# A fused attention-and-MLP kernel: slot-side softmax transposed without its normalisation, the slot reads divided by the sums afterwards

## The chip, the cores and the metric

The kernel runs on one core of a Trainium2 chip. The metric is the device time of one execution in microseconds, the median of several; lower is better.

## The reference

For each of B = 8 batches and H = 8 heads, `x` is [512, 64] and `state` is [32, 64]. Tokens read from the state slots and slots read from the tokens; both results are concatenated to 544 rows per batch, and the heads side by side give 512 columns. A two-layer network with the activation s r^2 + b follows. In short:

```python
scores  = x @ state.T / 8;   xread = softmax(scores, over slots) @ state
scores2 = state @ x.T / 8;   sread = softmax(scores2, over tokens) @ x
X = concat([xread, sread])               # 8 batches x 544 rows, 512 columns
r = relu(X @ w_in)                       # w_in [512, 2048]
out = (s * r * r + b) @ w_out            # w_out [2048, 512]
```

`scores2` is the transpose of `scores`, so one matrix of exponentials E serves both softmaxes: column sums give the token side, row sums give the slot side.

## The kernel before, in words

Slots stand on the partitions: four heads of 32 slots make 128 partitions, the 512 tokens are the columns, and two groups g = 0, 1 hold the eight heads. For each batch b:

- `T_mm` writes the scores (T) to PSUM, and `E_exp` on ScalarE makes E[g] = exp(T / 8) in fp16 with `accum_out`, which leaves the sums over tokens in `rs`, one column for each half of the tokens.
- Token side: `D_mm` multiplies E by a block matrix of ones (D), `D_ln` and `D_exp` on ScalarE make R = 1/D, and `a4_mul` on VectorE makes a4 = E R, the normalised weights. `M_mm` forms M = state @ w_in, four column chunks c of 512 for each batch, cast to fp16 by `M_cast` on ScalarE or VectorE. `h_mm` then multiplies a4 by M: h(b,f), f = 0 to 15, are blocks of 128 hidden units for 512 tokens, each of two matmuls of 512 columns.
- Slot side: `q_rec` adds the two halves of `rs` and takes the reciprocal q, `a2_mul` on VectorE multiplies E by q, `aT_dma` on SP transposes the product (aT), `V_mm` multiplies aT by x (V, in PSUM), `V_copy` casts V to `sr`, and `sr_dma` on SP transposes sr into `srdT`. When all eight batches have done so, `h_mm` with the name "sr" runs the slot rows through w_in itself.
- The network's second half: `relu` (ScalarE mostly), `square` (VectorE) make g. Batch 0 is multiplied by w_out directly in groups of four f: `rows_mm`, here called rows(b, rr, part), each four matmuls of 512 columns, closed by `rows_out` on VectorE. The other batches, and the slot rows, use a seven-product scheme: `pair_sums` (pd) and `weight_sum` (u) on VectorE, `step_mm` on TensorE with 256-column matmuls, `step_out` on VectorE (c), `step_put` to memory.

Batches 0 and 1 arrive as fp32 on SP's queue and are cast and transposed on the engines (`cast_x`, `xT_mm`, `xT_copy`). Everything else is loaded by GpSimd's queue, which casts on the way; its order is the string `SEQ`: four chunks of w_in (wi), four of w_out (wo), 512 KB each as fp16, then x of batches 2 and 3.

The order of instructions on each engine is not written down by hand. The class `Plan` holds every operation with an engine, a guessed duration, a key, what it needs and makes and which buffers it takes, and lays them out greedily by ready time and key; `after` is an earliest time. The constants `K` set the keys. The result is only an order: on the chip each engine runs its queue in that order and waits on semaphores, and nothing holds an operation back until its planned time. PSUM has four banks for attention tiles (T, D, M, V and the transposes share the pool "att"), two for h and two for outputs; the four are handed out again in the order in which they were given back.

T_mm, M_mm, V_mm and the bias sum run TensorE in tiles of 32 columns or 64 rows; the others use the full array. The prediction calls a run of such tiled products, between others, an excursion. "warm" matmuls are fillers that the plan puts into TensorE's queue before 14 us.

The kernel's core for the slot side:

```python
nc.vector.tensor_scalar(a[f"a2{g}"], a["E"][g], a["q"][:, g : g + 1], None, ALU.mult)   # a2_mul
nc.sync.dma_start_transpose(a["aT"][:, g], a[f"a2{g}"])                                 # aT_dma
copy_on(e, A[b]["sr"], A[b]["V"].rearrange("p g d -> p (g d)"))                         # V_copy
```

## Time and profile before

| | us |
|---|---|
| median of 5 runs | 212.17 (211.1, 211.1, 212.17, 212.8, 212.9) |
| profiled execution, its own time | 211.49 |
| its span, first to last instruction | 209.7 |
| TensorE busy | 201.5 |
| VectorE busy | 174.7 |
| ScalarE busy | 138.0 |
| GpSimd busy | 42.0 |

The granted TensorE clock was 0.998 of full speed. In the profile, PE is TensorE's matmuls, PEld its weight loads, DVE VectorE, ACT ScalarE, POOL GpSimd, SP the queue that issues most transposes. A line such as "L213 PE MATMUL h<-a,M" names the line of the code (L213 is the helper `mm`), the engine, and the tiles written and read. "Busy" adds an instruction's whole duration; two neighbours on ScalarE or VectorE overlap by about a tenth of a microsecond, so the spacing of their starts is shorter than the duration.

### The profile page before, as it was taken

To read this page: it belongs to the slowest core of one execution; us is meant where nothing else is said; L and a number is where in the kernel's file an instruction comes from. 1 tells how busy PE (TensorE), PEld (TensorE's weight loads), DVE (VectorE), ACT (ScalarE), POOL (GpSimd) and SP (SyncE) were. 2 spreads that over 40 slices of the span, in tenths; PEclk is the share of its full clock that TensorE was granted. 3 is DMA by queue.
4 is the path that set the end of the run, shared out by engine and by line. 5 is a ranking of instruction groups with operands and counts; after the bars stand their busy time and mean duration, and the time that the engine had idled before them with its cause. 6 is when DMAs were issued, how large, how long until landed. Compare 5 with 4: busy or idle time off the path is not lost.

```text
span 209.7 us, 4984 instructions
## 1 busy us (share of the span) xinstructions
PE 201.5 (96%) x1961; PEld 131.2 (63%) x1961; DVE 174.7 (83%) x415; ACT 138.0 (66%) x311; POOL 42.0 (20%) x65
## 2 busy tenths in 40 slices
PE   7896999999999999999999999999999999999993
PEld 3432434435667676667767667766766777888882
DVE  2489899998799998999998998989898988828872
ACT  4797999814986698868695959675967554116500
POOL 0760000262050224013231214111101111200000
PEclk9999999999999999999999999999999999999999
DMA  6999999579759764952495449741212110320132
GB/s 202 293 181 206 208 211 147 118 174 169 154 122 131 128 158 95 127 134 73 77 149 107 112 100 140 96 125 53 75 34 100 50 53 28 105 76 3 53 125 75
DMA packets 42344, 25.00 MB, mean 119 GB/s; under 512 B 26448, under 2 KB 40528, under 8 KB 42320
## 3 DMA queue, kind: packets, MB, share of 16 engines
q0 software_dynamic: 12896, 14.68, 36.4%
q1 hardware_dynamic: 29136, 9.84, 23.7%
q8 instruction: 15, 0.25, 0.5%
q10 hardware_dynamic: 288, 0.16, 0.3%
q14 instruction: 9, 0.07, 0.1%
HBM read 17.33 MB, written 8.91 MB: 125 GB/s over the span
## 4 chain that ended last, share of the span: by engine, by line
PE 86%; DMA 7%; DVE 3%; POOL 1%; SPq 0%; ACT 0%; issue 0%
PE o L213 47%; PE h L213 25%; DMA wi<-in_moe_w_in_dram 5%; PE Mps L213 4%; PE h_sr L213 3%; PE osr L213 3%; DMA xf<-in_x_dram 2%; DVE g L810 2%; PE V L213 1%; PE D L213 1%; PE T L213 1%; PE wsum_ps L213 0%; SPq L255 0%; POOL wi L361 0%; POOL wo L371 0%; DVE osb L953 0%
## 5 line engine op out<-in xcount | busy, mean ns | idle before, releaser
L804 ACT ACTIVATE g<-h 128x512 f16<-128x512 f32 x125 | 73.0, 601 | 31.1 <-PE h L213 29.9
L213 PE MATMUL h<-a,M 128*128 128x512 f16 x256 | 73.9, 379 | 0.0
L810 DVE TENSOR_TENSOR g<-g 128x512 f16<-128x512 f16 x128 | 52.1, 425 | 4.2 <-ACT g L804 2.8
L213 PEld LDWEIGHTS <-pd 128*128 128x128 f16 x448 | 43.0, 98 | 18.3 <-issue 2.6
L213 PEld LDWEIGHTS <-g 128*128 128x128 f16 x400 | 38.4, 98 | 23.2 <-issue 2.6
L213 PE MATMUL o<-u,pd 128*128 128x256 f16 x336 | 45.8, 273 | 0.0
L213 PE MATMUL o<-wo,g 128*128 128x256 f16 (+1 forms) x288 | 45.5, 296 | 0.2 <-DVE osb L953 0.2
L1061 POOL DMA_DIRECT2D out_dram<-c x24 | 16.4, 683 | 102.6 <-DVE c L1049 97.6
L305 ACT CAST M<-Mps 128x512 f16<-128x512 f32 x51 | 28.7, 594 | 7.6 <-PE Mps L213 7.2
L213 PEld LDWEIGHTS <-M 128*128 128x128 f16 x256 | 24.3, 98 | 10.9 <-issue 3.1
L1049 DVE SCALAR_TENSOR_TENSOR c<-o,sb_cols,bias_bc 128x512 f32<-128x512 f32 x28 | 21.0, 749 | 6.1 <-PE o L213 5.5
L1049 DVE SCALAR_TENSOR_TENSOR c<-o,sb_cols,c 128x512 f32<-128x512 f32 x21 | 15.8, 751 | 5.7 <-PE o L213 5.2
L826 DVE TENSOR_TENSOR pd<-g 128x1024 f16<-128x1024 f16 x28 | 19.2, 686 | 0.3
L213 PE MATMUL o<-u,g 128*128 128x256 f16 x112 | 15.7, 273 | 0.0
L548 ACT ACTIVATE E<-T 128x256 f16<-128x256 f32 x32 | 11.9, 385 | 4.9 <-PE T L213 4.9
L213 PE MATMUL o<-wo,pd 128*128 128x256 f16 x112 | 15.0, 273 | 0.0
L384 POOL DMA_DIRECT2D xn<-in_x_dram x18 | 13.9, 813 | 0.0
L837 DVE TENSOR_TENSOR pd<-g,pd 128x512 f16<-128x512 f16 x28 | 11.8, 422 | 0.5
L793 ACT ACTIVATE g_sr<-h_sr 128x128 f16<-128x128 f32 x16 | 4.4, 277 | 11.8 <-PE h_sr L213 11.8
L835 DVE TENSOR_TENSOR pd<-g,pd 128x512 f16<-128x512 f16 x28 | 11.8, 420 | 0.3
L574 ACT ACTIVATE R<-D 128x512 f16<-128x512 f32 x16 | 9.6, 597 | 0.5
L567 ACT ACTIVATE D<-D 128x512 f32<-128x512 f32 x16 | 9.5, 595 | 0.0
(78 smaller groups left out, 164.7 us busy)
## 6 DMA issues: line engine op xcount, KB each, us to landing
out_dram<-c POOLq DMA_DIRECT2D x24, 256.0 KB, 2.5
xf<-in_x_dram SPq DMA_DIRECT2D x8, 256.0 KB, 5.3
wi<-in_moe_w_in_dram POOLq DMA_DIRECT2D x4, 512.0 KB, 11.5
wo<-in_moe_w_out_dram POOLq DMA_DIRECT2D x4, 512.0 KB, 14.9
xn<-in_x_dram POOLq DMA_DIRECT2D x16, 128.0 KB, 3.6
xn<-in_x_dram POOLq DMA_DIRECT2D x2, 512.0 KB, 14.7
out_dram<-osb POOLq DMA_DIRECT2D x4, 256.0 KB, 3.2
out_dram<-c SPq DMA_DIRECT2D x4, 256.0 KB, 2.4
```

Of the source, the lines that this page charges most:

```text
L213: return nc.tensor.matmul(out, lhsT, rhs, start=start, stop=stop, tile_position=tp, is_transpose=is_transpose, skip_group_check=True,)
L305: nc.scalar.copy(dst, src)
L384: nc.gpsimd.dma_start(out=xn[b][:, h0:h1].rearrange("p h c d -> p h (c d)"), in_=x[b, h0:h1].rearrange("h (q c) d -> q h (c d)", q=P),)
L548: nc.scalar.activation(a["E"][g][:, 256 * m : 256 * m + 256], a["T"][m][:, g, :], AF.Exp, scale=scale, accum_out=a["rs"][:, g, m : m + 1],)
L574: nc.scalar.activation(A[b][f"R{g}"], A[b][f"D{g}"], AF.Exp, scale=-1.0)
L804: nc.scalar.activation(g_of(name, f), OSB["h", name, f], AF.Relu)
L810: ENG[e].tensor_mul(g_of(name, f), g_of(name, f), g_of(name, f))
L826: nc.vector.tensor_tensor(pd[:, :, 0:2], g4[:, :, 1:2, :].to_broadcast((P, 2, 2, t)), g4[:, :, 0:4:3, :], ALU.subtract,)
L835: nc.vector.tensor_tensor(pd[:, :, 2], g4[:, :, 3], pd[:, :, 0], ALU.subtract)
L837: nc.vector.tensor_tensor(pd[:, :, 3], g4[:, :, 2], pd[:, :, 2], ALU.subtract)
L1049: nc.vector.scalar_tensor_tensor(t, src, s_bc, add, ALU.mult, ALU.add)
L1061: ENG[e].dma_start(dst[:, rows:SCH:2, hD * h : hD * h + hD], SN[b, name])
```

## The change

E itself is transposed, not E q. `a2_mul` and its tiles are gone, `V_copy` multiplies by q on its way out of PSUM. For batches 0 and 1 the exponentials no longer accumulate; instead `E_sum` on ScalarE reads each E tile later with a Copy that accumulates, its output unused. There are four E buffers for each g instead of three, and four q. The load order and all keys are others, so the order of every engine's queue is other too. The transpose's `after` is now `K["a2"]` + 2 g.

```diff
--- before.py
+++ after.py
@@ -128,6 +128,7 @@
                     if kind == "load":
                         done = max(channel, end + 2.0) + span
                         channel = max(channel, done)
+                        done += 0.8
                     elif kind == "tp" and e == "SP" and now < channel + 4.0:
                         done = end + max(span, min(8.0, 6.0 - 0.75 * (now - channel)))
                         channel = max(channel, now + 2.0) + 1.1
@@ -273,12 +274,12 @@
         xn[b] = xpool.tile([P, H, SCH, D], FP16, name=f"xn_{b}", tag="xn")
 
     K = dict(
-        h1=10.0, hs=1.7, M0=-5.0, M1=2.6, T1=1.9, x2=11.8, T2=30.2, D2=21.8, M2=30.7, V0=21.7, V1=28.2, u=16.2,
-        us=7.8, pd1=8.7, o0=13.5, o2=20.2, w=38.4, r=-3.3, T=-9.7, D=1.8, Mb=8.9, V=11.6, S=3.7, S0=2.2,
-        E=-13.4, L=-7.1, E0=-7.3, L0=-7.0, E1=-0.2, L1=-6.1, a4=4.0, Mc=5.2, pd=14.0, solo=5.4, f0=-0.5,
-        f1=15.2, mc=0.2, hsr=-5.9, Ssr=-0.1, jE00=-8.0, jE01=3.2, jL00=1.3, jL01=1.0, jR00=-2.8, jR01=0.3,
-        jE10=3.3, jE11=7.2, jL10=-6.0, jL11=7.6, jR10=7.2, jR11=-3.9, jM0=2.4, jM1=1.3, xc=-10.2, a2=30.7,
-        lx=8.3, la=12.9, lb=7.4,
+        h1=11.4, hs=0.6, M0=-4.5, M1=1.5, T1=-0.1, x2=24.5, T2=21.0, D2=30.7, M2=36.0, V0=28.2, V1=21.7, u=8.1,
+        us=10.1, pd1=2.0, o0=16.0, o2=26.0, w=25.1, r=0.5, T=-11.4, D=7.3, Mb=3.9, V=7.6, S=3.4, S0=-1.2,
+        E=-7.1, L=-5.0, E0=-6.7, L0=6.1, E1=-7.0, L1=-5.1, a4=-9.7, Mc=4.9, pd=14.6, solo=6.8, f0=0.4, f1=15.4,
+        mc=0.9, hsr=-10.9, Ssr=-2.4, jE00=-6.1, jE01=5.2, jL00=3.0, jL01=14.6, jR00=-0.1, jR01=-6.7, jE10=3.3,
+        jE11=-6.4, jL10=-5.2, jL11=5.1, jR10=-1.5, jR11=7.4, jM0=0.0, jM1=0.3, xc=-8.5, a2=30.8, lx=6.3, la=7.6,
+        lb=9.4, rs=28.3,
     )
     A = {b: {"E": {}, "a4": {}} for b in range(B)}
     G, PD, U, SN, OSB = {}, {}, {}, {}, {}
@@ -308,9 +309,9 @@
 
     plan = Plan(
         {
-            "att": 4, "h": 2, "xn": 6, "xT": 2, "stT": 2, "E0": 3, "E1": 3, "R0": 1, "R1": 1,
-            "a40": 2, "a41": 2, "M": 2, "aT": 3, "a20": 2, "a21": 2, "sr": 4, "g": 8, "pd": 7,
-            "u": 4, "osb": 6, "q": 2, "rs": 3,
+            "att": 4, "h": 2, "xn": 6, "xT": 2, "stT": 2, "E0": 4, "E1": 4, "R0": 1, "R1": 1,
+            "a40": 2, "a41": 2, "M": 2, "aT": 3, "sr": 4, "g": 8, "pd": 7,
+            "u": 4, "osb": 6, "q": 4, "rs": 3,
         },
         solo=K["solo"],
     )
@@ -390,7 +391,7 @@
 
     gate = konst.tile([P, 2], FP16, name="gate")
     nc.gpsimd.tensor_copy(gate, xf_part(0, 2)[:, 0, 0:2])
-    SEQ = "wi0 wo0 wi1 wi2 wo1 wo2 wi3 wo3 x2 x3"
+    SEQ = "wi0 wi2 wo1 wi1 wo0 wi3 wo2 wo3 x2 x3"
     seq = [(t[:-1], int(t[-1])) for t in SEQ.split()]
     for n, it in enumerate(seq):
         key = -40 + n
@@ -543,15 +544,20 @@
             a = A[b]
             if "rs" not in a:
                 a["rs"] = apool.tile([P, NG, 2], FP32, name=f"rs_{b}", tag="rs", bufs=3)
-            a["E"][g] = apool.tile([P, S], FP16, name=f"E_{b}_{g}", tag=f"E{g}", bufs=3)
+            a["E"][g] = apool.tile([P, S], FP16, name=f"E_{b}_{g}", tag=f"E{g}", bufs=4)
             for m in range(2):
+                kw = {} if b < 2 else dict(accum_out=a["rs"][:, g, m : m + 1])
                 nc.scalar.activation(
-                    a["E"][g][:, 256 * m : 256 * m + 256],
-                    a["T"][m][:, g, :],
-                    AF.Exp,
-                    scale=scale,
-                    accum_out=a["rs"][:, g, m : m + 1],
-                )
+                    a["E"][g][:, 256 * m : 256 * m + 256], a["T"][m][:, g, :], AF.Exp, scale=scale, **kw
+                )
+
+        return fn
+
+    junk = konst.tile([P, S], FP16, name="junk")
+
+    def E_sum(b, g):
+        def fn(e):
+            nc.scalar.activation(junk, A[b]["E"][g], AF.Copy, accum_out=A[b]["rs"][:, g, 0:1])
 
         return fn
 
@@ -607,17 +613,10 @@
     def q_rec(b):
         def fn(e):
             a = A[b]
-            a["q"] = apool.tile([P, NG], FP32, name=f"q_{b}", tag="q")
-            nc.vector.tensor_tensor(a["q"], a["rs"][:, :, 0], a["rs"][:, :, 1], ALU.add)
-            nc.vector.reciprocal(a["q"], a["q"])
-
-        return fn
-
-    def a2_mul(b, g):
-        def fn(e):
-            a = A[b]
-            a[f"a2{g}"] = apool.tile([P, S], FP16, name=f"a2_{b}_{g}", tag=f"a2{g}")
-            nc.vector.tensor_scalar(a[f"a2{g}"], a["E"][g], a["q"][:, g : g + 1], None, ALU.mult)
+            a["q"] = apool.tile([P, NG], FP32, name=f"q_{b}", tag="q", bufs=4)
+            if b >= 2:
+                nc.vector.tensor_tensor(a["q"], a["rs"][:, :, 0], a["rs"][:, :, 1], ALU.add)
+            nc.vector.reciprocal(a["q"], a["q"] if b >= 2 else a["rs"][:, :, 0])
 
         return fn
 
@@ -626,7 +625,7 @@
             a = A[b]
             if "aT" not in a:
                 a["aT"] = apool.tile([P, NG, SCH, P], FP16, name=f"aT_{b}", tag="aT", bufs=3)
-            nc.sync.dma_start_transpose(a["aT"][:, g], a[f"a2{g}"])
+            nc.sync.dma_start_transpose(a["aT"][:, g], a["E"][g])
 
         return fn
 
@@ -650,7 +649,12 @@
     def V_copy(b):
         def fn(e):
             A[b]["sr"] = apool.tile([P, NG * D], FP16, name=f"sr_{b}", tag="sr", bufs=4)
-            copy_on(e, A[b]["sr"], A[b]["V"].rearrange("p g d -> p (g d)"))
+            nc.vector.tensor_tensor(
+                A[b]["sr"].rearrange("p (g d) -> p g d", g=NG),
+                A[b]["V"],
+                A[b]["q"].unsqueeze(2).to_broadcast((P, NG, D)),
+                ALU.mult,
+            )
 
         return fn
 
@@ -730,7 +734,7 @@
             Dps = ("att", f"D{b}{g}")
             rs = ("rs", f"rs{b}")
             add(
-                AC(0.73), kT + kE + g + K.get(f"jE{b}{g}", 0.0), E_exp(b, g), [("T", b, g)] + ([("E", b, 0)] if g else []),
+                AC(0.73 if b >= 2 else 0.55), kT + kE + g + K.get(f"jE{b}{g}", 0.0), E_exp(b, g), [("T", b, g)] + ([("E", b, 0)] if g else []),
                 [("E", b, g)], Tb + [Eb, rs],
             )
             add(PEt(0.22), kD, D_mm(b, g), [("E", b, g)], [("D", b, g)], [Eb, Dps, Rb, a4b])
@@ -738,14 +742,13 @@
             add(AC(0.53), kD + kL + g + K.get(f"jR{b}{g}", 0.0), D_exp(b, g), [("Dl", b, g)], [("R", b, g)], [Dps, Rb])
             add(DV(0.34), kD + K["a4"], a4_mul(b, g), [("R", b, g)], [("a4", b, g)], [Eb, Rb, a4b])
             add(
-                DV(0.27), kD + 4, a2_mul(b, g), [("q", b)], [("a2", b, g)],
-                [Eb, ("q", f"q{b}"), (f"a2{g}", f"a2{b}{g}")], after=K["a2"],
-            )
-            add(
-                ("SP", 1.2), kD + 5, aT_dma(b, g), [("a2", b, g)],
-                [("aT", b, g)], [(f"a2{g}", f"a2{b}{g}"), ("aT", f"aT{b}")], ("tp", K["la"] if b < 2 else K["lb"]),
-            )
-        add(DV(0.25), kD + 4, q_rec(b), [("E", b, 0), ("E", b, 1)], [("q", b)], [rs, ("q", f"q{b}")])
+                ("SP", 1.2), kD + 5, aT_dma(b, g), [("E", b, g)] + [("q", b)] * 0,
+                [("aT", b, g)], [Eb, ("aT", f"aT{b}")], ("tp", K["la"] if b < 2 else K["lb"]), after=K["a2"] + 2 * g,
+            )
+            if b < 2:
+                add(AC(0.63), K["rs"] + 2 * b + g, E_sum(b, g), [("E", b, g)], [("sum", b, g)], [Eb, rs], after=24.0)
+        q_need = [("sum", b, 0), ("sum", b, 1)] if b < 2 else [("E", b, 0), ("E", b, 1)]
+        add(DV(0.25), kD + 4, q_rec(b), q_need, [("q", b)], [rs, ("q", f"q{b}")])
         M_b = ("M", f"M{b}")
         for c in range(4):
             mp = [("att", f"M{b}{c}{g}") for g in range(2)]
@@ -765,7 +768,7 @@
             PEt(0.22), kV, V_mm(b), [("aT", b, 0), ("aT", b, 1)], [("V", b)],
             [V_b, ("aT", f"aT{b}"), xn_b], tiled=True,
         )
-        add(DV(0.22), kV, V_copy(b), [("V", b)], [("sr", b)], [V_b, ("sr", f"sr{b}")])
+        add(DV(0.25), kV, V_copy(b), [("V", b), ("q", b)], [("sr", b)], [V_b, ("sr", f"sr{b}"), ("q", f"q{b}")])
         add(("SP", 1.2), kV, sr_dma(b), [("sr", b)], [("srT", b)], [("sr", f"sr{b}")], ("tp", 4.0))
```

## The prediction

> **What bounds the kernel now.** First the page, engine shares and the 40 slices: TensorE is busy 96% of the span, and from the fifth slice (21 us) its digit is 9 to the last but one.
>
> ```profile
> PE 201.5 (96%) x1961; PEld 131.2 (63%) x1961; DVE 174.7 (83%) x415; ACT 138.0 (66%) x311; POOL 42.0 (20%) x65
> ...
> PE   7896999999999999999999999999999999999993
> ...
> DVE  2489899998799998999998998989898988828872
> ```
>
> A busy matmul row can hide stalls, so next the sums by stretch (columns: length, then PE, PEld, DVE, ACT, POOL busy, granted clock, DMA, GB/s) and TensorE's timeline from 12 us:
>
> ```profile
> 12.80:24.64 11.84, 9.69 (x95) 3.71 (x95) 10.36 (x26) 10.47 (x26) 1.03 (x2) 1.00 1.22 202
> 24.64:42.35 17.71, 17.44 (x126) 7.05 (x119) 16.62 (x44) 16.34 (x33) 1.90 (x4) 1.00 1.04 160
> ...
> 60.00:180.00 120.00, 120.00 (x1208) 83.11 (x1206) 108.15 (x247) 86.39 (x182) 26.09 (x38) 1.00 0.52 99
> ```
>
> ```profile
> 12.80 0.41 PE L213 MATMUL Mps<-wi,stT 64*32 64x512 f16 x8
> ...
> 13.94 0.73 PE L213 MATMUL Mps<-wi,stT 64*32 64x512 f16 x8 [0.30 <-ACT M L305]
> 14.61 1.04 PE L213 MATMUL h<-a,M 128*128 128x512 f16 x4
> ...
> 18.88 0.41 PE L213 MATMUL Mps<-wi,stT 64*32 64x512 f16 x8 [1.85 <-DMA wi<-in_moe_w_in_dram]
> ...
> 22.48 1.03 PE L213 MATMUL o<-wo,g 128*128 128x512 f16 x4
> 23.34 1.03 PE L213 MATMUL h<-a,M 128*128 128x512 f16 x4
> 24.30 0.41 PE L213 MATMUL Mps<-wi,stT 64*32 64x512 f16 x8
> ```
>
> Four 512-column matmuls start 0.86 us apart from the next four (22.48 to 23.34): 0.217 each, the pace for the rest of the kernel. At 60 to 180 us PE is busy 120.00 of 120.00 us and VectorE idle for 12. So VectorE and ScalarE work saved after 25 us buys nothing by itself; only TensorE stalls count. Those that a change could remove are: the 1.85 us for the third weight load at 18.88, about 0.8 at 13.4 to 14.3 for PSUM, 0.12 before 29.20 (the fourth wi), and 0.39 at 41.8 to 42.35 for an output bank. About 3 us in all.
>
> **The change, part by part.** Durations:
>
> ```profile
> L548 ACT ACTIVATE E<-T 128x256 f16<-128x256 f32 x32 | 11.9, 385 | 4.9 <-PE T L213 4.9
> L548 ACT ACTIVATION_READ_ACCUMULATOR E<-T 128x1 f32 x32 | 6.6, 208 | 0.0
> ...
> L620 DVE TENSOR_SCALAR a<-E,q 128x512 f16<-128x512 f16 x16 | 5.5, 365 | 0.2
> ...
> L307 DVE CAST sr<-V 128x128 f16<-128x128 f32 x8 | 2.3, 284 | 0.0
> ```
>
> *a2_mul goes.* 16 x 365 ns = 5.5 us of VectorE (4.2 by their spacing, two take 0.61 from 31.20), plus two q additions of 157 ns. Off the path: worth 0 directly. The planner spends it: 23 M_casts instead of 13 now stand in VectorE's queue (685 ns each, about +6.1 us by spacing 0.61), ten fewer in ScalarE's (594 ns). VectorE's sum barely moves.
>
> *V_copy becomes a multiply* from PSUM by a broadcast q. Not in the trace: at least the 284 ns of the cast; at most the 484 ns that a PSUM operation of 256 columns takes (c_sr). I take 300. Behind V(7) the transposed result landed at 185.8 and h_sr needed it at 187.3, so 1.5 us of cover; in the new order V(7) to h_sr is 28 slots of 0.217, 6.1 us, against about 0.6 for VectorE and 4.0 for the transpose. Worth 0.
>
> *Transposes read E directly.* Same 16 transposes, same size (median 2.6 us), issued on SP a few places earlier; for later batches they no longer wait for q. The new order uses that: V(b) for b = 3 to 6 stands about 15 slots (3.3 us) earlier in TensorE's queue. Landing against need from before's times: V(3) is needed near 84.8 us and its last transpose leaves SP near 72; V(2) near 68 and 58. Seven us or more of cover: 0. SP's moved sr_dma stands ahead of three xT transposes of 1.3 us each, which have about 10 us to T(b+2): 0.
>
> *Sums of batches 0 and 1 on ScalarE.* Removed: 8 accumulator reads, each putting 0.09 us between two ACTIVATEs (9.11 to 9.20). Added: four Copy activations of 128x512 with an accumulator. Nearest rows: ACT COPY xT<-xTps 128x512, 579 ns, 0.48 by spacing, plus a read of 0.09: 0.59 each, 2.35 us. Bounds: 0.48 (the read hidden) and 0.79 (both durations end to end, 579 + 208); at 0.79 the four take 3.2, which the cover below still nearly holds. They stand between relus at about 31 to 38 us, and h banks (two) wait behind them. Cover: from 24.5 us to relu of h(1,12) the new ScalarE queue holds 17 relus, 6 M_casts and 4 sums, 17 x 0.49 + 6 x 0.48 + 2.35 = 13.6 us, for 16.1 us of TensorE work. 2.4 us spare: 0. Without that cover each would cost up to 0.59. Here a rule speaks against the change: the Trainium skill, "ScalarE: Activation LUTs", section "Rules for kernel authors", sends copies, adds and multiplies to VectorE. By the rows it is right on price: 0.26 on VectorE (a2_mul's spacing) against 0.59. By the rule the sum would lose 4 x 0.59 = 2.35 us on the engine that feeds TensorE; by the rows only what exceeds 2.4 us of slack, nothing. I follow the rows.
>
> *Load order.* POOL now asks wi0, wi2, wo1, wi1, wo0, wi3, wo2, wo3, x2. In the trace these eight equal 512 KB loads land one behind another, at 12.30, 15.71, 18.83, 21.10, 23.68, 26.20, 29.16, 31.75 us (x2 34.41). I keep the slots and exchange the names: wi2 15.71, wo1 18.83, wi1 21.10, wo0 23.68.
>
> *The start, walked down the new queues with these spacings.* ScalarE takes over the cast of the last x piece (0.52), so batch 0's last reciprocal exp ends near 13.44 instead of 13.16. M(0,0) now takes that bank: 13.5, not 12.80. E of batch 1, without reads and before the M_cast, runs 13.33 to 14.50 (before 13.79 to 15.27). M(1,0) takes its banks at 14.55; M_casts end at 15.0 to 15.7; the D matmuls follow; h(0,0) starts at 15.44 instead of 14.61. From there ScalarE is the pace: M_cast, ln, exp, ln, relu, exp, relu in a row. M(0,2) goes at 16.4 (wi2 is there), h(0,3) waits for the relu of h(0,1) until 17.75, M(1,2) 18.3, h(1,0) 18.7, h(1,3) ends at 20.8. M(0,1) then waits for wi1, 21.15. So the long load wait shrinks to 0.3, but 0.8 us have gone to the late start and about 1.3 to ScalarE. From 21.15 the queue is dense: M(0,1), h(0,8), h(0,9), M(1,1), h(0,4), h(0,5) to 23.67, wo0 landed at 23.68, first rows group to 24.6.
>
> At 24.6 the new order has done 12 h tiles, 1 rows group and 6 M; before had at 24.64 done 10 h, 2 rows groups and 6 M, and a rows group is two h. Equal. After that no new stall appears: wi3 (26.20) is needed at 27.3, banks for rows(0,2) are free at 40.1 for 40.55. The 0.12 and the 0.39 go, 0.51 together. Mode changes: each excursion to the tiled matmuls costs 0.2 (0.09 going, 0.12 back); the new queue has 31 against 29, but the two more lie before 24.6 and are in the walk; 23 remain in both. An added warm-up matmul stands in idle time.
>
> **Sum:** -0.04 - 0.51 = **-0.55 us** on the profiled execution: 211.49 to 210.9 (span 209.7 to 209.15, the 1.8 around it unchanged). The five times' median is 212.17, 0.7 above the profiled one, so the predicted median is **211.6**.
>
> **Rivals.**
> *A, the start gains nothing back.* The walk allows 0.1 us for each hand-over (M(0,0) ended at 13.21, its cast began at 13.30); ten that take 0.2 would push h(1,3) past 21.15, and the weight stream may run at its slow early pace (3.1 to 3.4 us a load), wi1 at 22.0. Price +0.9 to +1.4, less 0.55: 212.5 to 213.0. For it: 1.3 us of ScalarE-paced TensorE in the walk. Against: 0.3 us slack. Still within 1%.
> *B, the load wait really goes.* If wi1 lands by 19.5 and ScalarE keeps up, 1.85 + 0.51 = 2.36 us: 209.8. For it: 8 h tiles ready ahead of wi1. Against: it is now the fourth load.
> *C, slower: VectorE's M_casts hold PSUM.* In batches 3 to 7 V(b) follows M(b+1,0) by 16 slots (3.5 us; before 31) and takes the bank of an M_cast that is VectorE's. Two casts are 1.2 and hand-overs 0.2, which leaves 2.1 us for whatever stands in VectorE's queue ahead. It decides from a backlog of 2.1; at 2.7 (an output of 0.67, a pd of 0.61, four squares of 0.34) it costs 0.6 in each of five batches: -0.55 + 3.0, 214.6. For it: VectorE 90% busy there, ten more casts. Against: such waits are 0.7 us in all of before.
> *D, the sums reload tables.* The trace has one ACT_TABLE_LOAD (1283 ns) for exp, ln, relu and copy together, and the same skill page, "Table sets: the hidden batching unit", has copy in every set; no run here shows this accumulating Copy. Three groups, two loads each: 7.7 us less 2.4 of slack: near 217. Taken together with C.
>
> **Chances.** Forecast 0.52, A 0.24, B 0.10, C with D 0.14. A measurement of this kernel tells about 1% (its five times spread over 0.85%). Faster by over 1% (below 210.05): B, 0.10. Slower (above 214.3): 0.14. Same: 0.76. The range takes the forecast's own (211.0 to 212.2), A, and the nearer parts of B and C: 209.8 to 214.0.
>
> **What would show it.** Right: the first M(0,1) waiting shortly on a load near 21.1 us, h(0,0) near 15.4, no PE wait over 0.3 us between 25 and 50, four ACT reads of about 0.6 us near 31 to 38 with PE dense beside them, sr<-V,q near 0.3 us, PE 120 of 120 at 60 to 180 us. Wrong: PE waits on ACT g at 31 to 38 (the sums), on DVE M in later batches (C), a second ACT_TABLE_LOAD (D), or a first M on wi1 without a wait before 20 us (B).

## The result and the profile after

The changed kernel takes 211.56 us in the median (210.86 to 213.28) where the kernel before, on the same chip in the same hours, took 211.96 (210.8 to 213.88). The ratio is 0.9981, 95% interval 0.9968 to 0.9994: 0.2% faster. Ratios leave out the few executions over 1.5% above the fastest of their kernel (three of before's 242, one of e10's); counts of executions below take all. The profiled execution's span went from 209.7 to 209.2 us.

The page of the changed kernel, engine shares and the slices of PE and DVE:

```profile
PE 202.5 (97%) x1962; PEld 131.4 (63%) x1962; DVE 175.9 (84%) x406; ACT 135.6 (65%) x302; POOL 41.1 (20%) x65
...
PE   7998999999999999999999999999999999999993
...
DVE  2569999998779898899989998999899989867762
```

The fourth slice (15.7 to 20.9 us), where the stand for wi1 was, went from 6 to 8, the second from 8 to 9. VectorE, which lost 16 multiplications, is as busy as before (175.9 against 174.7 us).

The sums by stretch, same columns as before (length, then PE, PEld, DVE, ACT, POOL busy, granted clock, DMA, GB/s):

```profile
12.80:24.64 11.84, 10.57 (x81) 3.67 (x80) 10.46 (x23) 11.38 (x25) 1.18 (x2) 1.00 1.23 207
24.64:42.35 17.71, 17.71 (x117) 7.47 (x114) 17.10 (x45) 14.21 (x31) 2.55 (x5) 1.00 1.08 175
...
60.00:180.00 120.00, 120.00 (x1238) 82.40 (x1237) 109.79 (x242) 81.30 (x171) 23.67 (x35) 1.00 0.55 97
```

In the second stretch TensorE is now busy for all of its 17.71 us (before 17.44): the two stalls of 0.12 and 0.39 us are gone. The third stretch is unchanged. The opening, TensorE's timeline (start, length, and in brackets the idle time before it and what ended it):

```profile
14.02 0.68 PE L214 MATMUL Mps<-wi,stT 64*32 64x512 f16 x8 [0.42 <-ACT E L550]
...
15.20 1.03 PE L214 MATMUL h<-a,M 128*128 128x512 f16 x4
16.16 0.41 PE L214 MATMUL Mps<-wi,stT 64*32 64x512 f16 x8
...
17.51 0.59 PE L214 MATMUL h<-a,M 128*128 128x512 f16 x2 [0.34 <-ACT g L807]
18.03 0.41 PE L214 MATMUL Mps<-wi,stT 64*32 64x512 f16 x8
...
19.77 1.08 PE L214 MATMUL h<-a,M 128*128 128x512 f16 x4 [0.36 <-ACT g L807]
20.78 0.41 PE L214 MATMUL Mps<-wi,stT 64*32 64x512 f16 x8
...
23.67 1.02 PE L214 MATMUL o<-wo,g 128*128 128x512 f16 x4
24.53 1.03 PE L214 MATMUL h<-a,M 128*128 128x512 f16 x4
```

The 1.85 us stand for a weight load is no longer there; what remains are stands of 0.3 to 0.4 us that ScalarE ends. h(0,0) starts 0.6 us later than before (15.20 against 14.61). When before's stand for wi1 has just ended, the changed kernel is about 1 us ahead at equal work; by 24.5 us they are level: the work that before has done at 24.64 us (10 h tiles, 2 rows groups, 6 M) the changed kernel equals at 24.53 (12, 1 and 6, a rows group being as long as two h tiles). At 34 us it is 0.57 ahead, and 0.48 at the end.

The groups by form (busy us, mean ns):

```profile
L308 DVE CAST M<-Mps 128x512 f16<-128x512 f32 x23 | 15.1, 684 | 0.5 <-PE Mps L214 0.4
L560 ACT ACTIVATE junk<-E 128x512 f16<-128x512 f16 x4 | 2.5, 630 | 0.0
L652 DVE TENSOR_TENSOR sr<-V,q 128x128 f16<-128x128 f32 x8 | 2.3, 284 | 0.1
...
L259 ACT ACT_TABLE_LOAD x1 | 1.3, 1283 | 1.7 <-PEq L1143 1.7
...
L560 ACT ACTIVATION_READ_ACCUMULATOR junk<-E 128x1 f32 x4 | 0.8, 198 | 0.0
```

23 M_casts on VectorE instead of 13; the multiply from PSUM costs what the cast did, 284 ns; a late sum is 630 ns and a read; one table load, as before.

### The profile page after: what moved, and what is told of

Read it like the earlier page. It is cut to its first block, busy times and chain, and to the rows that moved or that the text cites. A ratio compares the mean times of both kernels' runs of the same rounds, so it can differ in the third digit from the quotient of the medians.

```text
span 209.2 us, 4981 instructions
## 1 busy us (share of the span) xinstructions
PE 202.5 (97%) x1962; PEld 131.4 (63%) x1962; DVE 175.9 (84%) x406; ACT 135.6 (65%) x302; POOL 41.1 (20%) x65
## 4 chain that ended last, share of the span: by engine, by line
PE 87%; DMA 9%; POOL 2%; SPq 0%; DVE 0%; issue 0%
PE o L214 49%; PE h L214 24%; DMA wo<-in_moe_w_out_dram 7%; PE Mps L214 4%; PE h_sr L214 3%; PE osr L214 3%; DMA xf<-in_x_dram 2%; PE V L214 1%; PE D L214 1%; POOL wi L362 1%; PE T L214 1%; PE wsum_ps L214 0%; SPq L256 0%; POOL wo L372 0%; DVE c_sr L1052 0%; PE bias_ps L214 0%
## 5 line engine op out<-in xcount | busy, mean ns | idle before, releaser
L813 DVE TENSOR_TENSOR g<-g 128x512 f16<-128x512 f16 x128 | 52.7, 424 | 5.1 <-ACT g L807 3.3
L214 PE MATMUL o<-u,pd 128*128 128x256 f16 x336 | 48.8, 273 | 0.0
L214 PEld LDWEIGHTS <-M 128*128 128x128 f16 x256 | 24.6, 98 | 12.8 <-issue 3.6
L306 ACT CAST M<-Mps 128x512 f16<-128x512 f32 x41 | 22.8, 594 | 4.7 <-PE Mps L214 4.7
L214 PE MATMUL o<-u,g 128*128 128x256 f16 x112 | 17.2, 273 | 0.0
L308 DVE CAST M<-Mps 128x512 f16<-128x512 f32 x23 | 15.1, 684 | 0.5 <-PE Mps L214 0.4
L214 PE MATMUL o<-wo,pd 128*128 128x256 f16 x112 | 15.5, 273 | 0.0
L550 ACT ACTIVATE E<-T 128x256 f16<-128x256 f32 x32 | 11.4, 385 | 2.5 <-PE T L214 2.5
```

What stands on the lines that cost most here:

```text
L214: return nc.tensor.matmul(out, lhsT, rhs, start=start, stop=stop, tile_position=tp, is_transpose=is_transpose, skip_group_check=True,)
L306: nc.scalar.copy(dst, src)
L308: ENG[e].tensor_copy(dst, src)
L550: nc.scalar.activation(a["E"][g][:, 256 * m : 256 * m + 256], a["T"][m][:, g, :], AF.Exp, scale=scale, **kw)
L813: ENG[e].tensor_mul(g_of(name, f), g_of(name, f), g_of(name, f))
```

## The experiments

Each ratio is to the kernel before, run beside it on the same chip; e1 to e4, e5 to e8, e9 to e11 and e12 ran on four different chips. Before's own median was 211.96 us beside the changed kernel and 211.75, 211.64, 211.65 and 212.17 beside these four groups, so differences of medians across groups hold to about half a us, and the ratios count. Two questions were open. Which part of the change is worth what? And why do the times of before spread so far upwards? A quarter of its 242 executions lie above 212.5 us, against 4 of the changed kernel's 58.

| kernel | median us | ratio, 95% interval |
|---|---|---|
| changed | 211.56 | 0.9981, 0.9968 to 0.9994 |
| changed, second series (e8) | 211.2 | 0.9982, 0.9952 to 1.0012 |
| e1, late sums twice | 213.98 | 1.0121, 1.0094 to 1.0148 |
| e2, VectorE +3.2 us | 211.21 | 0.9981, 0.9965 to 0.9997 |
| e3, VectorE +12.7 us | 219.61 | 1.0388, 1.0348 to 1.0427 |
| e4, weights in the old order | 217.27 | 1.0272, 1.0243 to 1.0301 |
| e5, sums back in the exps | 211.88 | 1.0014, 0.9996 to 1.0032 |
| e6, new arithmetic, before's queues | 212.9 | 1.0047, 1.0024 to 1.007 |
| e7, no late sums | 211.43 | 0.9996, 0.9978 to 1.0014 |
| e9, before, wait filled | 211.63 | 1.0001, 0.998 to 1.0022 |
| e10, e6, wait filled | 212.4 | 1.0027, 1.0006 to 1.0048 |
| e11, e4, wait filled | 215.37 | 1.016, 1.0108 to 1.0212 |
| e12, e10 with 16 dead VectorE instructions | 211.56 | 0.9973, 0.9951 to 0.9996 |

**e1: the late sums taken twice.** In `E_sum` of the changed kernel:

```diff
             nc.scalar.activation(junk, A[b]["E"][g], AF.Copy, accum_out=A[b]["rs"][:, g, 0:1])
+            nc.scalar.activation(junk, A[b]["E"][g], AF.Copy, accum_out=A[b]["rs"][:, g, 0:1])
```

> The changed kernel with each of the four late sums taken twice, in the same place: 4 x 0.62 us more on ScalarE between 31 and 40 us. The prediction's cover was pooled (2.4 us spare in ScalarE's queue up to the relu of h(1,12); its profile shows 3.5 us idle between 24.6 and 42.4): by that nothing moves, +0.0 to +0.2 us. Rival: the cover is local, because only two h banks stand between TensorE and the relus; then the first pair's 1.24 us puts the relu of h(0,12) at 33.7 instead of 32.5, h(0,14) waits for its bank until 34.4 instead of 33.4, and the run is 1.0 to 1.3 us longer (ratio to before 1.003 to 1.005 instead of 0.998).

213.98 us, 2.4 us above the changed kernel (3.0 by the ratios). Between the two profiled executions the span grew by 3.0 us, of which 0.24 are there before the first sum; so 2.8 us come from added ScalarE work of 3.0 (4 sums, 0.75 us apart where one follows another). A shared reserve of 2.4 us would have left 0.6. e1's waits (us in total, times, longest):

```profile
PE h L214 <- ACT g L808: 1.9, 3, 1.2
...
PE o L214 <- DVE osb L957: 1.0, 1, 1.0
```

and where they stand in its timeline:

```profile
34.85 1.08 PE L214 MATMUL h<-a,M 128*128 128x512 f16 x4 [1.17 <-ACT g L808]
...
43.32 1.89 PE L214 MATMUL o<-wo,g 128*128 128x512 f16 x8 [0.95 <-DVE osb L957]
```

ScalarE's timeline shows why at 34.85: the sums run in pairs, so twice the pair is four in a row, at 31.33, 32.09, 32.84 and 33.59, and the next relu starts at 34.22. TensorE has only two h banks to run ahead in, and both wait for that relu. The second wait is further off: q_rec on VectorE stands waiting for the last sum, with rows_out queued behind it, and TensorE needs the bank that rows_out frees. The reserve is what two h banks cover, at that place; it isn't what ScalarE has to spare over 18 us. Yet the step expected of the local cover, 1.0 to 1.3 us in all, is only the first of the two waits; the second, by way of VectorE and an output bank, was not foreseen.

**e7: the late sums left out.**

```diff
-            nc.scalar.activation(junk, A[b]["E"][g], AF.Copy, accum_out=A[b]["rs"][:, g, 0:1])
+            return
...
+            if b < 2:
+                nc.vector.memset(a["q"], 1.0)
+                return
```

> The changed kernel without the four late sums and with nothing in their place (the sums of batches 0 and 1 are left out and q is set to one for them). Theory (in single dose the sums fit into the cover of the two h banks): +0.0 us against the changed kernel, ratio 0.998. Rival (they cost their own time, as the added ones did): up to -2 us, ratio 0.989.

211.43 us, ratio 0.9996: no faster than the changed kernel. In single dose the four sums are hidden, and the next four (e1) hardly at all: the change uses nearly all of its cover. The profile agrees where the sums stand: 0.12 us ahead of the changed kernel up to 20 us, 0.67 behind from 21 us because in that execution wi1 landed at 21.50 us and not at 20.56, and 0.67 still at the end: leaving the sums out gained nothing between.

**e5: the sums back where they were,** as `accum_out` of the exps of batches 0 and 1, everything else as changed:

```diff
-                kw = {} if b < 2 else dict(accum_out=a["rs"][:, g, m : m + 1])
+                kw = dict(accum_out=a["rs"][:, g, m : m + 1])
...
-            nc.scalar.activation(junk, A[b]["E"][g], AF.Copy, accum_out=A[b]["rs"][:, g, 0:1])
+            return
```

> The changed kernel with one part undone: batches 0 and 1 accumulate their sums in the exponentials again, the four late sums are gone, all queues stand as they are. Theory (the move keeps ScalarE's chain at the start short): E(0) and E(1) grow by 0.19 and 0.38 us, M(1,0) and the chain behind it go 0.4 to 0.55 later up to a4(1,1), the load slots of wi1 and wo0 absorb 0.2 to 0.3 of it, +0.3 us in all, ratio 0.999 to 1.000. Rival (the late sums stood on the path, as the run with two of each hints, where every added microsecond was paid): the four late sums gone give back up to 2 us, ratio 0.990 or less.

211.88 us, ratio 1.0014, 0.3% above the changed kernel, with intervals that just part from the changed kernel's first series and overlap its second. The eight reads stand in the ScalarE-paced opening: TensorE is 0.54 us later at M(1,0) and 0.67 at h(0,3), and stays 0.67 later up to 20 us (then 1.2, as wi1 landed 1.4 us later in that execution). So moving the sums is worth about 0.4 to 0.7 us: e5's mean is 211.92, against 211.46 of e8 and 211.50 of e7 on the same chip.

**e2 and e3: VectorE's relief taken back.** Behind each `a4_mul` of batches 2 to 7 stand one (e2) or four (e3) dead multiplications of a2_mul's shape:

```diff
+            for _ in range(1 if b >= 2 else 0):        # e3: 4
+                nc.vector.tensor_scalar(junk_v, A[b]["E"][g], sb_cols[:, 0:1], None, ALU.mult)
```

> The changed kernel with the removed multiply put back as work whose result nobody reads: one tensor_scalar of 128x512 on VectorE behind each a4_mul of batches 2 to 7, 12 x 0.26 = 3.2 us. Theory (only TensorE's stalls count, VectorE's relief was worth nothing): +0.0 us, ratio 0.998, PE still 120.0 of 120.0 between 60 and 180 us. Rival (the gain is VectorE's relief): the gain goes, +0.4 us, ratio 1.000 or more.

> As the run with the multiply put back, but four of them behind each a4_mul: 48 x 0.26 = 12.7 us more of VectorE, in bursts of 1.06. VectorE's idle time in the changed kernel is 10.2 us of the 120 between 60 and 180 by durations, and nearly twice that by the spacing of starts. Theory: by spacing there is still room, so +0 to +1.5 us, from bursts that delay a square or a cast. Rival C of the prediction (casts on VectorE sit on TensorE's path with 2.1 us to spare, and a pair of bursts is 2.1): PE waits on DVE in every batch, +2 to +5 us.

e2 takes 211.21 us, ratio 0.9981, the changed kernel's own: 3.2 us more on VectorE cost nothing. Its profiled span was 210.4 all the same, and its waits on TensorE name the cause:

```profile
PE Mps L214 <- DMA wi<-in_moe_w_in_dram: 1.2, 2, 0.8
```

In that execution wi1 landed at 21.81 us and not at 20.56, and everything behind it is 1.2 us late: the weight stream, not the added work.

e3 takes 219.61 us, +8.1, far more than both theories gave. Its waits and one of their places:

```profile
PE o L214 <- DVE g L816: 6.1, 5, 1.3
```

```profile
77.29 0.39 PE L214 MATMUL o<-wo,g 128*128 128x256 f16 x2 [1.01 <-DVE g L816]
```

TensorE waits for squares (DVE g), five times 1.0 to 1.3 us, not for M_casts as rival C had it. The dead work comes in bursts of eight behind a4_mul, and what stands behind a burst is the square that step_mm needs. VectorE's slack over six batches lies between 3.2 and 12.7 us; an estimate, if each us beyond it costs one, is 4.6 (12.7 - 8.1). How much of the 8.1 comes from the bursts and how much from the sum was not separated.

**e4: the weights in the old order.** The changed kernel with the load steps asking for wi0, wo0, wi1, wi2, wo1, wo2, wi3, wo3 as before:

```diff
+    ASK = [(t[:-1], int(t[-1])) for t in "wi0 wo0 wi1 wi2 wo1 wo2 wi3 wo3 x2 x3".split()]
...
-            load(key, 0.8, 2.6, load_wi(it[1]), [it], after=6.6)
+            load(key, 0.8, 2.6, (load_wi if ASK[n][0] == "wi" else load_wo)(ASK[n][1]), [it], after=6.6)
```

> The changed kernel's queues, but GpSimd asks for the weights in the old order (wi0 wo0 wi1 wi2 wo1 wo2 wi3 wo3). Theory (loads land one after another in fixed slots, and the new queue of TensorE fits the new slots alone): M(0,2) at 16.2 us waits for wi2, now fourth, until 20.6; the later work is denser because ScalarE has caught up; +2.5 to +3.5 us in all, ratio 1.010 to 1.015. Rival (the weight order is hidden anyway, the start is paced by ScalarE): under +1 us.

217.27 us, +5.7 over the changed kernel (+6.2 by the ratios), about twice what was expected. The tile came as late as the exchange of names says:

```profile
21.16 0.63 PE L214 MATMUL Mps<-wi,stT 64*32 64x512 f16 x8 [4.84 <-DMA wi<-in_moe_w_in_dram]
```

but then the sums by stretch of e4 show something that no row of before has, in the granted clock (third number from the end):

```profile
16.40:21.16 4.76, 0.00 (x0) 0.00 (x0) 0.95 (x3) 1.64 (x4) 0.00 (x0) 0.85 1.23 204
21.16:25.30 4.14, 4.14 (x23) 1.11 (x24) 2.50 (x6) 1.20 (x3) 0.47 (x1) 0.50 1.21 198
25.30:30.00 4.70, 4.69 (x31) 1.61 (x30) 3.84 (x9) 4.26 (x9) 0.19 (x1) 0.86 1.23 215
```

After the stand TensorE ran at half its clock, h matmuls 0.427 us apart instead of 0.217. From the three means (0.85, 0.50, 0.86) the half clock held for 1.4 + 4.1 + 1.3 = 6.9 us. All four executions of e4 have it: their mean granted clocks are 0.981 to 0.984.

**e6: the new arithmetic alone,** on before's queues, keys and loads: no a2_mul, transposes of E, V times q.

```diff
             return                                     # a2_mul, in before a tensor_scalar
-            nc.sync.dma_start_transpose(a["aT"][:, g], a[f"a2{g}"])
+            nc.sync.dma_start_transpose(a["aT"][:, g], a["E"][g])
-            copy_on(e, A[b]["sr"], A[b]["V"].rearrange("p g d -> p (g d)"))
+            nc.vector.tensor_tensor(sr, A[b]["V"], q.unsqueeze(2).to_broadcast((P, NG, D)), ALU.mult)   # in short
```

> The kernel before, its queues and load order unchanged, with only the arithmetic of the change: a2_mul is left out, E is transposed, V is multiplied by q on its way out of PSUM (sums stay with the exponentials in every batch). Theory (the arithmetic alone is worth nothing, the gain is in the new order of the start): ratio 1.000 within 0.15%. Rival (VectorE's relief of 4.2 us or earlier transposes carry the gain): 0.998 or less.

212.9 us, ratio 1.0047: slower than before, and neither theory had that. Its sums by stretch:

```profile
18.80:20.04 1.24, 1.24 (x13) 0.48 (x13) 1.07 (x3) 0.90 (x2) 0.00 (x0) 0.95 1.23 203
20.04:23.00 2.96, 2.96 (x22) 0.73 (x21) 1.82 (x6) 1.61 (x3) 0.00 (x0) 0.50 1.24 207
23.00:25.00 2.00, 2.00 (x9) 0.82 (x8) 0.96 (x4) 1.44 (x4) 0.18 (x1) 0.92 1.23 202
```

The same 1.9 us stand for wi1 as before (it ends at 18.76), and after it, for 0.12 + 2.96 + 0.32 = 3.4 us, the half clock; TensorE is 1.47 us behind before by 22 us. Before's own profiled execution has the same stand and a clock of 1.00 after it. What differs between the two shows when the traces are cut into steps of 3.41 us that end where the clock changes. From 12 us on it changes in e6 at 19.91, 23.33 and, after the last matmul, 211.06 us; in before only after the last matmul, at 209.04. From 19.91 to 211.06 are 191.15 us, 56 such steps, and 56 steps ahead of 209.04 lies 17.89. The steps around the stand, e6 first, then before:

```profile
16.50:19.91 3.41, 1.55 (x14) 0.60 (x13) 3.19 (x9) 3.17 (x6) 0.00 (x0) 1.00 1.24 207
19.91:23.33 3.42, 3.42 (x24) 0.80 (x22) 2.28 (x7) 1.77 (x3) 0.00 (x0) 0.50 1.24 205
```

```profile
14.48:17.89 3.41, 2.54 (x17) 0.98 (x11) 3.11 (x8) 3.30 (x11) 0.00 (x0) 1.00 1.24 206
17.89:21.30 3.41, 2.42 (x32) 1.02 (x31) 3.07 (x8) 2.47 (x6) 0.00 (x0) 1.00 1.24 205
...
205.63:209.04 3.41, 0.48 (x5) 0.19 (x2) 0.62 (x2) 0.00 (x0) 0.00 (x0) 1.00 0.34 115
209.04:209.70 0.66, 0.00 (x0) 0.00 (x0) 0.00 (x0) 0.00 (x0) 0.00 (x0) 0.50 0.00 0
```

In e6 the whole stand falls into one step, TensorE is busy for 1.55 of 3.41 us in it, and the next step runs at half clock. In before the edge at 17.89 splits the stand, both steps are busy for 2.4 us or more, and the clock stays. Cut in the same way, all fourteen traces agree: at full clock, every step with TensorE busy for 1.67 us or more was followed by the full clock, every step with 1.55 or less by the half clock (e4's step from 16.33 to 19.75 us has 0.00). So in these traces what counts is not the length of a wait alone but where it falls between the edges, and the edges of two executions differ. The Trainium skill, "TensorE: Matmul & The Clock Gate", Part 1, describes such a gate: it judges TensorE's activity in windows of about 3.4 us that do not start with the kernel, and halves the clock after an idle one. The half clocks here, 3.4 us and e4's 6.9, are one such window and two. Its advice under "HAM oscillation", no idle gaps over about 3.4 us, is too mild for these traces: 1.9 us in one step was enough.

The half clock is not why e6 is slower than before. Every execution's mean granted clock is on record; one at 0.992 or less has had such a step (e6's profiled execution has 0.990, before's 0.998). That is 7 of e6's 21 and 16 of before's 66 beside it, no clear difference; and at full clock e6 takes 212.52 us in the mean, before 211.43. Those 1.1 us need another cause; e10 and e12 find most of it.

**e9, e10, e11: the wait filled.** Eight matmuls on zeros (1.73 us) go into TensorE's queue behind h(0,3), in the kernel before (e9) and in e6 (e10); 21 of them behind h(0,1) in e4 (e11):

```diff
                 mm(hps, L[k], Rr[k], start=(k == 0), stop=(k == n - 1))
+            if (name, f) == (0, 3):                    # e11: (0, 1), range(21)
+                for _ in range(8):
+                    mm(ob[1], warm[:, 0:P], warm)
```

> The kernel before with eight matmuls on zeros (0.217 us each, 1.73 us) put into TensorE's queue behind h(0,3), where it otherwise stands for 1.85 to 1.98 us waiting for wi1; nothing else is changed. Theory: part of the gain of the change is that no 2 us stand is left in the opening, because such a stand is followed, in some executions and not in others, by some 3 us at a granted clock of 0.50 (the run with the old order and the new arithmetic shows it at 20.0 to 23.0 us, the profiled execution of before doesn't). Then the filled kernel before loses its upper executions (a fifth to a quarter of them lie above 212.5 us, none or one in twenty should) and its median goes from 211.7 to about 211.2 us, ratio 0.997 (0.995 to 0.999), level with the changed kernel. Rival: the spread of before comes from the weight stream alone; then the matmuls on zeros change nothing, ratio 1.000 and the same upper executions. If the stream comes earlier than the eight matmuls end, they cost up to 0.2 us.

> The kernel with before's queues and loads and the new arithmetic (212.9 us, ratio 1.0047) with the same eight matmuls on zeros behind h(0,3). Theory: its 0.5% over before is the half clock after the wait, met more often there; filled, it falls to 0.998 (211.2 us), and the profile shows a granted clock of 1.00 between 18.8 and 25 us. Rival: the new arithmetic in the old order costs 0.5% in itself (the longer V_copy, the banks); then it stays at 1.004 to 1.005.

> The changed kernel's queues with the weights asked for in the old order (217.27 us, ratio 1.0272), with 21 matmuls on zeros (4.5 us) behind h(0,1), where it stands 4.84 us for wi2. Theory: of the 5.7 us over the changed kernel, 4.6 to 5.0 are the late tile itself and about 1.2 us the half clock that follows; filled, 215.9 to 216.2 us, ratio 1.020 to 1.022, clock 1.00 from 21 us on. Rival: the loss is all of it the late tile and what it drags; then 217.3 us and 1.027 again.

e11: 215.37 us, 1.9 less than e4 (2.4 by the ratios) with the tile just as late, and the clock is back, in all four executions (means of 0.996 to 1.00):

```profile
21.16:25.30 4.14, 3.88 (x29) 1.29 (x28) 3.11 (x8) 2.49 (x5) 0.19 (x1) 1.00 1.23 202
25.30:30.00 4.70, 4.70 (x35) 1.94 (x35) 4.63 (x12) 4.64 (x10) 0.19 (x1) 1.00 1.23 216
```

35 matmuls in the last stretch where e4 did 31, and 29 where it did 23. So of e4's 5.7 us, 1.9 were the clock and 3.8 the late tile (of 6.2 by the ratios, 2.4 and 3.8); expected were 1.2 and 4.6 to 5.0.

e9: 211.63 us, ratio 1.0001. The median did not fall to 211.2, as the theory had it, so that number was wrong. Above 212.5 us lie 2 of 22 executions, beside 11 of 43 of before in the same series; by the clock, 2 and 8 had a step at half clock. So few can be chance: e9 alone does not decide. Its timeline:

```profile
17.28 1.89 PE L213 MATMUL o<-warm 128*128 128x512 f16 x8
19.10 0.41 PE L213 MATMUL Mps<-wi,stT 64*32 64x512 f16 x8
19.44 1.04 PE L213 MATMUL o<-wo,g 128*128 128x512 f16 x4
```

wi1 landed at 19.02 in this execution, so the eight cost at most 0.08 here. At full clock e9's executions take 211.64 us in the mean, before's beside it 211.58.

e10: 212.4 us, ratio 1.0027, not clearly better than e6 (the intervals overlap), and not 0.998. One of its 22 executions has a mean clock of 0.992 or less. In the profiled one the steps of 3.41 us lie as in e6's (one from 16.48 to 19.89 us); with the stand filled, that step is busy throughout. The clock is at 1.00 throughout, and TensorE is ahead of before's by 0.24 us at the last matmul, and yet the span is 210.4 us against 209.7. The rest is behind the last matmul: the last store of c_sr landed 2.95 us after its issue, in e6 3.01, in before, the changed kernel, and in e1 to e5, e7 to e9 and e11 2.05 to 2.07. DMA issues of e10 from 206 us on (two stores, median of both), with the queues' packets:

```profile
q1 hardware_dynamic: 402, 0.36, 11.1%
q14 instruction: 1, 0.01, 0.2%
issues: line engine op xcount, KB each, median us to landing
out_dram<-c_sr SPq DMA_DIRECT2D x2, 128.0 KB, 2.5
```

One packet of 8 KB on the instruction queue starts at 207.94 us and takes 0.31, among the packets of that last store; some of the store's packets behind it take 0.09 to 0.17 us instead of at most 0.06. In e6 the same packet comes at 209.31. In the changed kernel, which has 463 VectorE instructions in its trace where e6 and e10 have 450 (all of them, also those that the page's busy count leaves out), it comes at 201.10, in before, with 471, at 193.74. The whole distribution of e10 is shifted, not its top: at full clock it takes 212.41 us in the mean, e9 on the same chip 211.64.

**e12: e10 with 16 dead one-column instructions on VectorE,** where a2_mul stood:

```diff
-            return
+            nc.vector.tensor_scalar(junk_q, A[b]["q"][:, g : g + 1], 1.0, None, ALU.mult)
```

> The filled kernel in the old order (212.4 us, ratio 1.0027) with one dead VectorE instruction of one column (a tensor_scalar of q into a junk tile, some 0.06 us) in each of the 16 places where a2_mul stood; nothing reads them. In the two kernels of the old order with the new arithmetic the last store of c_sr landed 2.95 and 3.01 us after its issue, in ten others 2.05 to 2.07; in these two a block of instructions (8 KB, 0.31 us) is fetched at 207.94 and 209.31 us, while that store is under way, and packets of the store that follow it take 0.09 to 0.17 us instead of at most 0.06. The changed kernel, with 463 VectorE instructions in the trace instead of their 450, fetches it at 201.1 us. Theory: the fetch falls into the store because the old-order kernels have fewer VectorE instructions; with 16 more it comes before 203 us, the last store lands in 2.06 us, the span is 209.5 us and the time 211.5 us, ratio 0.9985 (0.9965 to 1.0005). Rival: the late store or the 0.3% has another cause, and the ratio stays at 1.002 to 1.003 with the store at 2.9 to 3.0 us, or the store is back at 2.06 us and the time is no shorter.

211.56 us, ratio 0.9973 where it was 1.0027 without them, the intervals apart. Part of that is the half clock, which 10 of before's 27 executions beside it had and 2 of e12's 22; at full clock e12 takes 211.54 us in the mean, before beside it 211.73, so the 0.8 us that e10 had over before are gone. The block is fetched at 202.22 us, and the same view of e12 from 207 us on has no instruction packet, and the stores at 2.0 us:

```profile
q1 hardware_dynamic: 432, 0.39, 37.5%
issues: line engine op xcount, KB each, median us to landing
out_dram<-c_sr SPq DMA_DIRECT2D x2, 128.0 KB, 2.0
```

The profiled span itself, 210.7 us, is no shorter than e10's: in that execution wi1 landed at 20.02 us and not at 18.18, and TensorE is 1.2 us later to the end. So the new arithmetic costs nothing in itself. With the stand filled and the fetch out of the way, the old queues are as fast as the changed kernel (0.9973, 0.9951 to 0.9996, against 0.9981).

**e8: the changed kernel again,** beside e5 to e7.

> The changed kernel itself, beside the next three on one chip. 0.998 of before, as in the comparison. In its profile the places that the prediction's walk names (h(0,0), M(0,1), the first rows group) should come out within the jitter of the weight stream, which differed by 1.2 us between the profiled executions so far (the fourth load landed at 20.56 in one and at 21.81 in another): if that jitter moves the run's end one for one, the end follows the landing of the fourth and fifth load.

211.2 us, ratio 0.9982, span 209.3, TensorE's timeline within 0.1 us of the first.

**What the spread says.** Before's executions of all series: lowest tenth 210.99, highest tenth 213.00 us. The changed kernel's: 211.02 and 212.29. The best executions are equal; the gain is at the top. The granted clocks say why. For 163 of before's executions, those beside e1 to e12, the mean clock is on record, and it falls into two groups with nothing between: 0.984 to 0.992, and 0.996 to 1.00.

| executions | number | with a clock of 0.992 or less |
|---|---|---|
| before | 163 | 39 |
| e6, the same stand | 21 | 7 |
| e9, e10, e12, the stand filled | 66 | 5 |
| changed, e2, e5, e7, e8, no long stand | 124 | 1 |

Of before's 37 executions above 212.5 us in these series, 33 are in the low group. Its mean is 212.99 us, that of the 124 others 211.54: a step at half clock costs 1.45 us. A quarter of the executions (39 of 163) at that price makes 0.35 us in the mean; the mean gain of the change is 0.33 (211.95 to 211.62). At full clock the two kernels do not differ: 211.54 us in the mean for before, 211.59 for the changed kernel (57 of 58 executions), each to about 0.1; on the one chip where both have it on record (beside e8), 211.43 and 211.46. So the gain is the half clock that the changed opening avoids. What a stand does is shown by e4 against e11, 4 of 4 and 0 of 4, and by the table; why filled kernels still have 5 in 66 is open. That before's low group has its half clock where e6 has it is inferred: no profile is of one of these executions.

## Why the prediction was right, point by point

- **What bounds the kernel:** right. TensorE is busy 120.00 of 120.00 us at 60 to 180; e2 shows that VectorE work saved there buys nothing, and e12 that the arithmetic as such costs nothing.
- **a2_mul and V_copy:** right. The saved 5.5 us (the row's busy time; 16 x 365 ns would be 5.8, as neighbours overlap) went into ten more M_casts, and the multiply took 284 ns, the lower bound, where 300 was chosen.
- **Late sums:** zero was right, its reason was not. A sum is 630 ns and a read, 0.62 by spacing alone and 0.75 before a second one, not 0.59, still inside the bounds of 0.48 and 0.79. The term that failed is the cover: 2.4 us were worked out by pooling ScalarE's spare time from 24.5 us to the relu of h(1,12) (16.1 less 13.6 is 2.5, but that is not what failed), and e1, 2.8 us of span for 3.0 us of added work, shows that next to nothing was left. Cover lies in the two h banks at the place. So the zero was in part luck: nothing in the working showed that the four sums would just fit. The rule of the Trainium skill that was weighed there names relu, max, min, add and mul, not copies; for the adding, which this Copy does, it gave a loss of 2.35 us, and e7 shows none.
- **Load order:** right in kind. The eight loads landed in slots, with the names exchanged, at 15.17 (wi2), 18.10 (wo1), 20.56 (wi1) and 23.62 (wo0), where 15.71, 18.83, 21.10 and 23.68 were said. In the profiled executions of e2, e5 and e7, with the same load order, wi1 was 0.9 to 1.4 us later than in the changed kernel's, more than the walk's 0.3 us of slack: rival A's second reason happens, in single executions.
- **The walk through the start:** right to 0.4 us at each step: h(0,0) 15.20 for 15.44, M(0,2) 16.16 for 16.4, h(0,3) 17.51 for 17.75, M(1,2) 18.03 for 18.3, M(0,1) 20.78 for 21.15, the first rows group ending at 24.53 for 24.6. Level with before there, as said. The short wait of M(0,1) for wi1 did not come, as the tile landed 0.2 us before M(0,1) was reached; in e2 it came (0.8 us).
- **The two stalls behind it:** 0.12 and 0.39 us are gone; between the two profiled executions the span is 0.5 shorter where -0.55 was said. Over many executions this does not show: at full clock the means are 211.54 and 211.59. The profiled execution of the changed kernel, 211.02 us, is one of its fastest tenth; before's, 211.49, lies at the median of its full-clock executions. Where the half us goes in the others is open; the jitter of the weight stream, up to 1.4 us, is as large as what is looked for.
- **Median of 211.6:** measured 211.56, with some luck. The sum took 0.55 us of stalls off a median of 212.17; the kernel before measured 211.96 beside the changed one, the medians differ by 0.40, and that gain has another source. The prediction read the 1.85 us stand as idle time only, and carried the 0.7 us between before's profiled execution and its median over as a constant. It left out that such a stand can bring a step at half clock behind it: this is what lifts before's median over its full-clock executions, and what the change takes away. The forecast of little change was right in its grounds, since what moves off TensorE's path buys nothing and the opening comes out level; its last half us was not.
- **Rivals:** A and B did not come in the profiled execution: wi1 landed at 20.56, neither after the walk's need for it nor before 19.5. C needs VectorE to be behind; e3 shows that 12.7 us more is enough for that, and that squares, not M_casts, are hit. D is refuted by the one table load.

## What to carry to other kernels

Hidden work is hidden locally: count what the banks at that place let TensorE run ahead, not what an engine has to spare over a longer stretch; doubling the dose in one run tells you how much cover is left. Before a transfer order is judged by the length of a wait, look at the granted clock in the rows behind the wait: in e4 a third of the loss was the clock. One profile isn't enough for that, since the same 1.9 us stand had it in e6's and not in before's; sort the executions by their mean clock before asking what their spread is. And when a variant's TensorE is ahead but its span isn't, read the last store's landing time and the instruction queue before blaming the arithmetic.

## What the runs showed of the hardware that was not expected

- The granted clock follows steps of 3.41 us: half clock behind a step in which TensorE was busy for 1.55 us or less (e6, e4 and the ends of the traces), full clock behind 1.67 or more at full clock. A stand of 1.9 us is followed by it when it falls into one step (e6) and not when an edge splits it (before). It costs 1.45 us an execution, in 39 of 163 of before; matmuls on zeros in the stand bring that to 5 of 66.
- Where an instruction block of 8 KB was fetched while the last store ran, that store landed 0.9 us later (2.95 and 3.01 us against 2.05); 16 tiny instructions more on VectorE moved the fetch ahead of it, and the store was back at 2.0 us and the time 0.8 us lower.
- A late sum of 128x512 with accumulator on ScalarE: 630 ns and a read of 198; the next sum, into the same junk tile, starts 0.75 us later, a relu 0.62.
- The weight stream, 512 KB a load in about 2.5 us, comes up to 1.4 us later in some executions with one load order (wi1 at 20.56 and 21.95), and what hangs on it moves with it.
